# A softcap attention and max-out kernel: the first part of its written order of work made anew

## The chip, the cores and the metric

The kernel runs on one core of one Trainium2 chip. The metric is device time in microseconds (us) of one execution, the median of several. TensorE is called PE (its weight loads PEld), VectorE DVE, ScalarE ACT, GpSimd POOL, and SyncE SP, whose queue issues DMAs.

## The reference

```python
scores = scale * np.matmul(q, k.transpose(0, 1, 3, 2))      # 8 batches, 12 heads, 448 x 448, head_dim 64
scores = cap * np.tanh(scores / cap)                        # cap = 30
attn = np.exp(scores - np.max(scores, axis=-1, keepdims=True))
attn = attn / (np.sum(attn, axis=-1, keepdims=True) + 1e-09)
x = np.matmul(attn, v)                                      # heads side by side: 3584 x 768
g = np.maximum(x @ w1, x @ w2)                              # 768 -> 1024
out = g @ w_out                                             # 1024 -> 768, float32
```

## The kernel before

The heads are taken two at a time ("pairs" i, 48 of them) and the pairs two at a time ("quads" t, 24). For one pair q and k come in, are cast to bf16 and turned so that the head dimension lies on the partitions: for the first ten pairs by PE transposes, later by DMA transposes. The max-out is rewritten as max(x w1, x w2) w_out = relu(x (w1 - w2)) w_out + x (w2 w_out). So a first stage makes wd = w1 - w2 on DVE and wm = w2 w_out on PE ("premultiplication"), and the rest of the kernel uses those. The products of the max-out are "groups": stage 1 gives relu(x wd), stage 2 the output rows.

There is no scheduler at work: the string `ORDER` lists every step of the whole kernel, written out, and each step issues its instructions at once. Each engine executes its own instructions in the order of the list; an instruction waits for what it needs from other engines. The place of a step against steps of other engines has no effect, only its place among those of its own engine. The steps that matter here:

- `ld0` loads q or k of pairs 0 and 1 (k on SP's queue, q on ACT's), `cd` casts them (ACT, the very first k on DVE). `lk`, `lq`, `lv` load k, q, v, `lw1`, `lw2`, `lwo` the weights, all on POOL's queue with a cast.
- `dm` fills a tile for warming matmuls, `ms0` and `id` make the identity (DVE, then POOL), `ms` fills constants (DVE). `D b n` does warming matmuls on n blocks of 128 columns in bank b, four blocks a matmul; their result is not used.
- `Xh`, `X i b` turn pair i into bank b (PE, 28 transposes of 64 x 64), `XCh`, `XC` copy that out (DVE). `W c b` turns a piece of w2 (8 transposes), `WC` copies it out. `OP c half b` takes bank b for a premultiplication, `P c half n` does n of its 8 matmuls, `PC` copies it out.
- `S i j` are the scores of pair i, keys j (2 matmuls of 64 x 448, in one of two PSUM slots of the scores), `T` their tanh and `E` their exp (ACT). `L`, `TL`, `EL` are the same for the keys left over by 3 x 128.
- `Y` sums the exps with a matmul of ones, `Y1`, `Y2`, `Y3` invert the sums (DVE), `VL`, `V` multiply by v (in a slot of the scores), `N` normalizes (DVE; `N t 1` is two instructions). `A`, `B` add exps ahead of the sum (DVE).
- `O g b` takes bank b for group g, `M x y n` does n steps of the first 64 rows for group x and n of the other 64 rows for group y, side by side, `ev` copies a group out (DVE), `H`, `Hs` hand a bank from one half to the other, `sub` makes a piece of wd (DVE), `cr` is a DMA transpose (SP), `st` a store.

The eight PSUM banks are four for the two slots of the scores and four (0 to 3) that `X`, `W`, `OP`, `Y`, `O` and `D` share. A bank that is taken again is written only when its old content has been read; the instruction on PE waits for that.

```python
def mm_tile(bank):
    idle.pop(bank, None)
    return mm_psum.tile([P, 512], f32, name=f"mm{bank}", bufs=1)
def s_tile(turn, t):
    return s_psum.tile([P, 2, 512], f32, name=f"s{turn ^ (t % 2)}")
```

Lines of the profile: L289 to L292, L734 and L735 are `ms`, `dm`, `ms0`; L277 `id`; L303 `ld0`; L308 and L310 `cd`; L321 and L328 `lk`, `lq`; L352 `lv`; L360 `lwo`; L366 `lw2`; L393 `lw1`; L402 `sub`; L416 `W`; L420 `WC`; L431 `P`; L437 `PC`; L458 `X`; L463 `XC`; L471 `D`; L475 `cr`; L514 `S`; L519 `T`; L528 `L`; L532 `TL`; L536 `E`; L539 `EL`; L548 `A`; L553 `B`; L566, L570 and L573 `Y`; L578, L581 and L584 `Y1` to `Y3`; L600 `VL`; L606 `V`; L618 and L621 `N`; L645 `M`; L666, L700 and L702 `ev`.

Of the kernel before, what the change touches and what calls it, by code (L numbers as in the profile page):

```python
# [778 lines left out]
```

## Time and profile before

| | |
|---|---|
| median of 3 runs | 330.23 us (330.17 to 330.53) |
| profiled execution | 330.47 us, span of its trace 328.7 us |
| PE busy | 321.4 us (98%) |
| ACT busy | 281.4 us (86%) |
| DVE busy | 240.5 us (73%) |
| POOL busy | 161.8 us (49%) |
| DMA | 46.28 MB, mean 141 GB/s |

A row of a timeline has the start in us, the duration of the piece, the engine, the line, the operation, what it writes and reads with partitions x elements, the count of instructions merged into the piece, and in brackets the idle time of the engine before it and what ended that. A row of a stretch has its bounds, its length, then the busy time of each engine with the count of instructions, the granted clock, the busy share of the DMA engines and GB/s. A row of a DMA queue has packets, MB and the share of the 16 engines' time.

### The profile page before, as it was taken

Reading aid. Unit: us, or ns where it says so; the run is one execution under the profiler, and the core shown is the slowest. Engines: PE = TensorE matmul, PEld = TensorE weight load, DVE = VectorE, ACT = ScalarE, POOL = GpSimd, SP = SyncE. Lnnn points to the kernel's source line nnn. Section 1 sums busy time; section 2 is a strip of 40 time slices with the busy share of each in tenths; the row PEclk is TensorE's granted clock in tenths of the full one; section 3 lists DMA queues with packets and bytes.
Section 4 is the critical chain, followed back from the end, with each engine's and each line's share of the span. In section 5 each row is a group of like instructions: output and inputs, shape, how many; then the busy total and the mean of one; then the engine's idle time right before and its main releaser. Section 6 shows DMA issues by size and latency. Waiting matters only on the chain.

```text
span 328.7 us, 9775 instructions
## 1 busy us (share of the span) xinstructions
PE 321.4 (98%) x4139; PEld 185.1 (56%) x4139; DVE 240.5 (73%) x422; ACT 281.4 (86%) x278; POOL 161.8 (49%) x237
## 2 busy tenths in 40 slices
...
GB/s 188 200 201 224 207 161 182 107 133 122 204 184 106 104 205 196 108 111 175 164 167 70 217 138 185 112 157 157 190 114 76 216 161 47 2 50 98 0 98 96
DMA packets 134507, 46.28 MB, mean 141 GB/s; under 512 B 112320, under 2 KB 129472, under 8 KB 134464
## 3 DMA queue, kind: packets, MB, share of 16 engines
...
q10 hardware_dynamic: 448, 0.66, 0.6%
...
## 4 chain that ended last, share of the span: by engine, by line
PE 96%; DVE 2%; issue 0%
PE mm L645 61%; PE s L514 10%; PE s L606 9%; PE mm L431 4%; PE s L528 2%; PE mm L471 2%; PE mm L573 2%; PE s L600 2%; PE mm L640 1%; PE mm L458 1%; PE mm L416 1%; DVE xT L621 1%; PE mm L566 1%; DVE xT L618 0%; DVE qkT L463 0%
## 5 line engine op out<-in xcount | busy, mean ns | idle before, releaser
L519 ACT ACTIVATE e<-s 128x896 bf16<-128x896 f32 x144 | 125.7, 928 | 6.6 <-PE s L514 6.4
L536 ACT ACTIVATE e<-e 128x1792 bf16<-128x1792 bf16 (+2 forms) x72 | 122.7, 1712 | 0.0
L645 PE MATMUL mm<-wo_sb,gT 64*128 64x384 bf16 x864 | 115.2, 323 | 0.0
L645 PE MATMUL mm<-wm_sb,xT 64*128 64x384 bf16 x648 | 102.3, 322 | 0.0
L645 PE MATMUL mm<-xT,wd_sb 64*128 64x448 bf16 x768 | 97.3, 349 | 0.0
L328 POOL DMA_DIRECT2D kqs<-in_k_dram x76 | 54.7, 722 | 56.2 <-DMA qkT<-kqs 51.4
L645 PEld LDWEIGHTS <-gT 64*128 64x128 bf16 x864 | 58.7, 94 | 25.3 <-issue 0.9
L645 PEld LDWEIGHTS <-wd_sb 64*128 64x128 bf16 x768 | 48.9, 94 | 26.5 <-issue 2.0
L645 PEld LDWEIGHTS <-xT 64*128 64x128 bf16 x648 | 50.7, 94 | 18.3
L514 PE MATMUL s<-qkT 64*128 64x448 bf16 x288 | 52.8, 355 | 0.6 <-DVE xT L621 0.6
L352 POOL DMA_DIRECT2D vp<-in_v_dram x48 | 30.5, 639 | 38.2 <-PE s L514 28.0
L666 DVE TENSOR_SCALAR gT<-mm 128x448 bf16<-128x448 f32 x64 | 38.9, 617 | 8.7 <-PE mm L645 7.6
L328 POOL DMA_DIRECT2D kqs<-in_q_dram x38 | 35.1, 925 | 4.4 <-PE mm L458 2.8
L606 PE MATMUL s<-e,vp 128*32 128x448 bf16 x576 | 35.6, 354 | 0.0
L548 DVE TENSOR_TENSOR esum<-e 128x896 bf16<-128x896 bf16 x42 | 25.8, 617 | 9.9 <-ACT e L536 9.9
L621 DVE TENSOR_TENSOR xT<-s,inv 64x448 bf16<-64x448 f32 x48 | 29.9, 622 | 0.9
L548 DVE TENSOR_TENSOR esum<-esum,e 128x896 bf16<-128x896 bf16 x42 | 26.2, 623 | 5.9 <-ACT e L536 4.8
L514 PEld LDWEIGHTS <-qkT 64*128 64x128 bf16 x288 | 18.5, 94 | 20.3 <-issue 11.1
L700 ACT COPY osb<-mm 128x384 f32<-128x384 f32 x10 | 4.8, 478 | 26.9 <-PE mm L645 26.7
L702 DVE COPY osb<-mm 128x384 f32<-128x384 f32 x44 | 23.3, 553 | 5.2 <-PE mm L645 4.7
L553 DVE TENSOR_TENSOR esum<-esum,el 64x896 bf16<-64x896 bf16 x42 | 26.0, 619 | 1.2
L578 DVE STREAM_TRANSPOSE st<-mm 128x448 f32<-128x448 f32 x24 | 15.6, 649 | 13.0 <-PE mm L573 11.4
...
## 6 DMA issues: line engine op xcount, KB each, us to landing
...
```

The costliest lines, as they stand in the source:

```text
L328: nc.gpsimd.dma_start(out=to, in_=x)
L352: nc.gpsimd.dma_start(out=to, in_=x)
L514: scored[i, j] = nc.tensor.matmul(s[:, h, :S], k_of(t, o, h, j), q_of(t, o, h)).ins
L519: nc.scalar.activation(expo[i][:, 2 * j : 2 * j + 2, :], slots[i, j][:, :, :S], AF.Tanh, scale=scale / cap)
L536: nc.scalar.activation(e, e, AF.Exp, scale=float(cap))
L548: nc.vector.tensor_add(d, e[:, 0:2, :] if j == 1 else d, e[:, 2 * j : 2 * j + 2, :])
L553: nc.vector.tensor_add(d, d, left_e[t][r, :, :])
L606: nc.tensor.matmul(vals[t][place(m, u), u, :S], w[:, m, :], expo[2 * t + o][:, 2 * j + h, :], start=False, stop=(j == NJ - 1))
L621: nc.vector.tensor_mul(x[64 - r : 128 - r], vals[t][r : r + 64, u, :S], sums[t, 3][64 - r : 128 - r])
L645: ins = nc.tensor.matmul(self.ps, w[r], x[r], start=first, stop=self.at == [self.n, self.n]).ins
L666: nc.vector.tensor_relu(gT[b // 2][:, f, cs], ps)
L702: nc.vector.tensor_copy(o[:, hs], ps)
```

## The change

Only `ORDER` changes. The steps up to the first ones of group 11 (438 steps before, 428 after) stand in a new order, with new banks; behind them the steps are the same 1900, with the banks 0, 1, 2, 3 renamed to 3, 2, 0, 1. The steps of the first part are the same in kind and number, but for the warming matmuls (96 blocks of 128 columns before, 104 after) and for pieces cut differently. Among the fills, `dm` and `ms0` stand ahead of `ms`; on POOL's queue the loads of pairs 3 and 2 stand ahead of the identity, and w2 and w_out behind them. In the old order one bank is taken while the copy of its old content stands further back in the list (`OP 4 0 2` before `XC 8`); in the new one none is.

```diff
@@ ORDER @@
-ld0 q; ld0 k; ms; ms0; dm; cd k; ld0 q 1; ld0 k 1; id; lwo 0 0; lw2 3; lw2 2; lk 3 0; lq 3 0; lw2 1; lk 2 0;
-lq 2 0; cd q; D 3 24; Xh 0 0 0; Xh 0 1; cd k 1 1; cd q 1 1; XCh 0 1; XCh 0 0; D 3 4; X 1 1; S 0 0; S 0 1; D 0 5;
-XC 1; T 0 0; T 0 1; D 1 16; S 0 2; L 0; W 3 2; T 0 2; TL 0; D 1 22; S 1 0; S 1 2; D 3 1; W 2 3; EL 0; T 1 0;
-T 1 2; lwo 0 1; lq 4 0; lk 4 0; lw2 0; lv 0 0; lv 0 1; WC 3; WC 2; D 2 8; S 1 1; D 2 4; OP 3 0 0; P 3 0 4; X 3 3;
-D 1 8; D 2 2; W 1 2; D 1 2; OP 2 0 1; P 2 0 2; XC 3; X 2 3; WC 1; XC 2; P 2 0 2; OP 1 0 2; P 1 0 3; S 2 1; T 1 1;
-E 0 0 3; E 1 0 2; T 2 1; S 2 0; P 1 0 2; P 3 0 1; P 1 0 1; P 3 0 1; L 1; P 2 0 1; P 1 0 2; P 2 0 2; P 3 0 2;
-P 2 0 1; PC 1 0; PC 2 0; T 2 0; TL 1; E 1 2 3; S 2 2; S 3 0; T 2 2; T 3 0; W 0 2; X 4 1; VL 0; V 0 0 0 3; Y 0 3;
-V 0 1 0 3; S 3 1; lwo 1 0; lwo 1 1; lq 5 0; lv 1 0; lk 5 0; lv 1 1; lq 7 0; lw2 4; lq 6 0; lk 6 0; lk 7 0; lw2 5;
-lq 8 0; lk 8 0; lw1 4; WC 0; XC 4; Y1 0; Y2 0; Y3 0; N 0 0; N 0 1; PC 3 0; E 2 0 3; T 3 1; EL 1; E 3 0 2;
-OP 2 1 1; P 2 1 1; OP 0 0 2; P 0 0 1; P 2 1 1; P 0 0 3; OP 1 1 3; P 1 1 2; P 2 1 1; P 1 1 1; P 2 1 1; P 1 1 3;
-P 0 0 2; P 2 1 2; S 3 2; S 4 0; P 0 0 2; OP 0 1 0; P 0 1 2; P 2 1 1; P 1 1 2; P 2 1 1; PC 0 0; X 5 2; PC 1 1;
-PC 2 1; XC 5; T 3 2; T 4 0; E 3 2 3; lw1 2; lw1 0; lq 9 0; lv 2 1; lv 2 0; S 4 1; S 4 2; T 4 1; T 4 2; Y 1 3; L 2;
-W 4 2; OP 3 1 1; P 3 1 1; VL 1; V 1 0 0 1; V 1 1 0 2; V 1 0 1 2; V 1 1 2 3; V 1 0 2 3; Y1 1; Y2 1; Y3 1; N 1 0;
-N 1 1; WC 4; TL 2; E 4 0 3; S 5 0; X 6 3; P 3 1 7; T 5 0; EL 2; XC 6; PC 3 1; S 5 1; S 5 2; X 8 2; X 7 3; T 5 2;
-T 5 1; E 5 2 3; E 5 0 2; OP 4 0 2; P 4 0 1; W 5 1; S 6 1; S 6 0; T 6 1; T 6 0; XC 8; WC 5; sub 4 0; XC 7; P 4 0 3;
-OP 5 1 1; P 5 1 1; P 4 0 2; P 0 1 4; P 5 1 1; P 0 1 2; Y 2 3; L 3; P 4 0 1; P 5 1 1; S 6 2; P 5 1 2; P 4 0 1;
-P 5 1 2; TL 3; T 6 2; sub 2 0; PC 0 1; sub 0 0; Y1 2; Y2 2; Y3 2; PC 4 0; P 5 1 1; O 1 0; M 1 -1 1; S 7 0; VL 2;
-V 2 0 0 3; V 2 1 0 3; OP 5 0 2; P 5 0 8; N 2 0; N 2 1; PC 5 1; EL 3; E 6 0 3; T 7 0; lk 10 1; lk 9 0; lq 11 0;
-lv 5 2; lq 12 0; lw1 1; lw1 3; lk 12 0; lk 12 1; lq 10 0; lk 11 1; lv 3 1; lw1 5; lk 11 0; lk 10 0; lv 3 0; S 7 2;
-O 0 3; M 0 -1 3; S 7 1; M 0 -1 3; T 7 2; T 7 1; Hs 0; S 8 1; X 9 1; M 1 -1 2; M 1 0 3; S 8 0; A 3 0 1; PC 5 0;
-sub 1 0; XC 9; sub 3 0; A 3 0 2; T 8 1; E 7 0 2; T 8 0; O 2 1; M 2 0 3; L 4; OP 4 1 2; P 4 1 8; S 8 2; M 2 1 3;
-A 3 1 1; ev 0; B 3 0; PC 4 1; B 3 1; Hs 2; TL 4; E 7 2 3; T 8 2; S 9 0; O 3 3; M 3 1 3; M 3 2 3; O 4 2; M 4 2 3;
-T 9 0; EL 4; A 3 1 2; ev 1; sub 5 0; Hs 3; cr 5; M 4 3 1; S 9 1; Y 3 0; VL 3; V 3 1 0 1; V 3 0 0 3; V 3 1 1 3;
-M 4 3 2; lq 13 0; lv 4 0; lk 13 0; lv 5 1; lv 5 0; lk 15 0; lv 4 1; lk 13 1; lq 15 0; lk 14 0; Y1 3; Y2 3; ev 2;
-Hs 4; O 5 1; M 5 3 3; M 5 4 3; T 9 1; E 8 0 3; E 9 0 2; Y3 3; N 3 1; ev 3; Hs 5; O 6 0; M 6 4 3; M 6 5 3; S 10 0;
-O 7 3; M 7 5 3; Hs 6; N 3 0; ev 4; ev 5; S 9 2; M 7 6 3; Hs 7; T 10 0; T 9 2; S 10 2; O 8 1; M 8 6 3; M 8 7 1;
...
+ld0 k; ld0 k 1; ld0 q; ld0 q 1; dm; ms0; lk 3 0; lk 2 0; lq 3 0; id; D 3 8; ms; cd q; cd k; lq 2 0; lw2 2; lw2 3;
+lw2 1; D 3 24; Xh 0 0 0; Xh 0 1; cd k 1 1; cd q 1 1; XCh 0 1; XCh 0 0; D 3 5; X 1 1; S 0 1; S 0 0; XC 1; T 0 1;
+T 0 0; D 0 5; D 1 12; L 0; D 1 8; S 0 2; W 2 0; TL 0; T 0 2; S 1 0; X 3 2; D 1 26; X 2 1; S 1 2; T 1 0; E 0 0 3;
+T 1 2; lwo 0 0; lwo 0 1; lv 0 1; lw2 0; lv 0 0; lk 5 0; lq 5 0; lq 4 0; lk 4 0; lwo 1 0; lv 1 1; lwo 1 1; WC 2;
+XC 3; XC 2; S 1 1; W 3 3; W 1 2; D 0 16; S 2 1; WC 1; WC 3; T 1 1; E 1 2 3; T 2 1; S 2 0; OP 1 0 1; P 1 0 1;
+OP 3 0 3; P 3 0 3; OP 2 0 0; P 2 0 3; P 1 0 1; P 2 0 1; P 1 0 2; L 1; P 3 0 1; P 1 0 2; P 3 0 1; P 2 0 1; P 1 0 1;
+P 3 0 1; P 2 0 3; P 3 0 2; PC 3 0; PC 2 0; T 2 0; E 1 0 2; TL 1; EL 0; S 2 2; S 3 0; Y 0 2; P 1 0 1; W 0 0; T 2 2;
+T 3 0; VL 0; V 0 0 0 3; V 0 1 0 3; S 3 1; X 4 3; lv 1 0; lk 8 0; lw2 5; lq 6 0; lk 7 0; lk 6 0; lw2 4; lq 8 0;
+lw1 4; lq 7 0; lw1 2; lw1 0; lv 2 1; lv 2 0; WC 0; Y1 0; Y2 0; PC 1 0; Y3 0; XC 4; N 0 0; N 0 1; E 2 0 3; T 3 1;
+EL 1; E 3 0 2; X 5 0; OP 0 0 2; P 0 0 5; OP 1 1 3; P 1 1 4; P 0 0 1; OP 2 1 1; P 2 1 3; S 4 0; S 3 2; P 0 0 1;
+P 2 1 2; P 0 0 1; P 1 1 3; P 2 1 3; P 1 1 1; XC 5; PC 0 0; PC 2 1; PC 1 1; T 3 2; T 4 0; E 3 2 3; OP 3 1 2;
+P 3 1 2; S 4 1; S 4 2; Y 1 1; T 4 1; T 4 2; L 2; P 3 1 4; VL 1; V 1 0 0 3; V 1 1 0 3; TL 2; E 4 0 3; S 5 0;
+P 3 1 2; W 4 3; T 5 0; EL 2; Y1 1; Y2 1; Y3 1; N 1 0; N 1 1; WC 4; PC 3 1; X 6 1; X 8 0; S 5 1; S 5 2; W 5 2;
+XC 8; XC 6; sub 4 0; WC 5; T 5 1; T 5 2; OP 4 0 0; P 4 0 8; S 6 0; X 7 1; OP 0 1 3; P 0 1 8; S 6 1; E 5 0 2;
+T 6 0; E 5 2 3; T 6 1; PC 4 0; XC 7; sub 2 0; PC 0 1; S 6 2; OP 5 1 1; P 5 1 7; L 3; T 6 2; TL 3; E 6 0 3; Y 2 3;
+VL 2; V 2 0 0 3; V 2 1 0 3; S 7 0; OP 5 0 2; P 5 0 1; P 5 1 1; P 5 0 7; sub 0 0; Y1 2; Y2 2; Y3 2; N 2 0; N 2 1;
+PC 5 1; A 3 0 1; PC 5 0; T 7 0; EL 3; lw1 1; lk 9 0; lq 10 0; lk 11 0; lw1 3; lq 9 0; lk 11 1; lv 3 1; lq 11 0;
+lv 4 0; lv 3 0; lk 10 0; lw1 5; lk 10 1; O 0 0; M 0 -1 1; S 7 2; S 7 1; O 1 3; M 1 -1 1; M 0 -1 3; M 1 -1 1;
+M 0 -1 2; T 7 1; T 7 2; Hs 0; S 8 0; M 1 -1 1; M 1 0 3; S 8 1; X 9 2; OP 4 1 1; P 4 1 4; sub 1 0; sub 3 0; XC 9;
+E 7 0 2; T 8 1; T 8 0; P 4 1 4; L 4; O 2 2; M 2 0 2; S 8 2; M 2 0 1; M 2 1 3; A 3 0 2; A 3 1 1; B 3 1; PC 4 1;
+ev 0; B 3 0; Hs 2; TL 4; E 7 2 3; T 8 2; S 9 0; O 3 1; M 3 1 3; M 3 2 3; O 4 0; M 4 2 3; VL 3; T 9 0; E 8 0 3;
+A 3 1 2; ev 1; ev 2; sub 5 0; Hs 3; cr 5; V 3 0 0 1; Y 3 3; V 3 0 1 3; V 3 1 0 3; M 4 3 1; S 9 1; M 4 3 2; O 5 2;
+M 5 3 3; lk 12 1; lk 13 0; lv 5 3; lq 13 0; lv 6 2; lv 4 1; lv 5 1; lk 12 0; lq 12 0; lk 15 0; lq 15 0; lk 13 1;
+lq 14 0; lk 14 0; Hs 4; M 5 4 3; T 9 1; Y1 3; Y2 3; Y3 3; ev 3; N 3 1; N 3 0; Hs 5; O 6 3; M 6 4 3; M 6 5 3;
+O 7 1; M 7 5 3; S 10 0; Hs 6; ev 5; A 4 0 1; ev 4; M 7 6 3; S 9 2; Hs 7; cr 6; EL 4; E 9 0 2; T 10 0; T 9 2;
...
```

More of the change, by code (lines that the diff above doesn't have):

```diff
@@ new lines @@
+M 12 10 1; Hs 11; cr 7; M 12 10 1; M 12 11 1; B 5 0; M 12 11 1; T 12 1; M 12 11 1; S 12 2; H 10 2; B 5 1;
+M 10 11 1; T 12 2; M 10 11 5; E 11 2 3; st 0 0; M 10 11 2; O 13 0; M 13 11 1; ev 10; L 6; VL 5; A 5 1 2; TL 6;
+V 5 0 0 2; V 5 1 0 2; Y 5 3; E 12 0 3; V 5 0 2 3; V 5 1 2 3; Y1 5; S 13 0; M 13 11 1; lv 7 0; M 13 11 1; Y2 5;
+M 13 12 2; Y3 5; M 13 12 1; lv 7 1; M 13 12 3; N 5 0; M 13 12 1; lv 7 2; M 13 12 1; T 13 0; M 13 12 1; N 5 1;
+M 13 12 1; lv 7 3; M 13 12 1; O 14 3; M 14 12 2; EL 6; Hs 13; S 13 1; lk 18 0; M 14 12 1; M 14 13 1; ev 11;
@@ new lines @@
+V 6 0 0 2; V 6 1 0 2; Y 6 1; E 14 0 3; V 6 0 2 3; V 6 1 2 3; Y1 6; S 15 0; M 18 16 1; lv 8 0; M 18 16 1; Y2 6;
+M 18 17 1; Y3 6; M 18 17 1; lv 8 1; M 18 17 1; O 19 1; M 19 17 2; ev 16; Hs 18; lv 8 2; M 19 17 1; M 19 18 1;
+T 15 0; N 6 0; M 19 18 2; lv 8 3; O 20 2; M 20 18 2; EL 7; Hs 19; ev 17; M 20 18 1; lk 20 0; S 15 1; M 20 19 1;
+N 6 1; M 20 19 1; T 15 1; M 20 19 1; lk 20 1; O 21 0; M 21 19 3; Hs 20; M 21 20 1; lq 20 0; ev 18; M 21 20 1;
+S 15 2; S 16 0; ev 19; M 21 20 1; T 15 2; O 22 3; M 22 20 1; lk 21 0; M 22 20 1; A 7 0 1; Hs 21; M 22 20 1;
@@ new lines @@
+M 22 21 1; E 15 0 2; M 22 21 1; lk 21 1; ev 20; S 16 1; M 22 21 1; O 23 1; M 23 21 1; A 7 0 2; M 23 21 1; Hs 22;
+lq 21 0; M 23 21 1; M 23 22 2; ev 21; M 23 22 1; T 16 0; M 23 22 2; A 7 1 1; M 23 22 2; cr 9; M 23 22 1; T 16 1;
+M 23 22 1; B 7 0; S 16 2; M 23 22 2; B 7 1; O 24 2; M 24 22 1; T 16 2; M 24 22 2; H 23; M 24 23 1; H 22 2;
+E 15 2 3; M 24 23 2; M 22 23 1; L 8; VL 7; A 7 1 2; TL 8; V 7 0 0 2; V 7 1 0 2; Y 7 0; E 16 0 3; V 7 0 2 3;
+lk 22 0; V 7 1 2 3; Y1 7; S 17 0; M 22 23 1; lv 9 0; M 22 23 1; Y2 7; M 22 23 2; Y3 7; M 22 23 1; lv 9 1;
@@ new lines @@
+M 22 23 2; O 25 0; M 25 23 1; N 7 0; M 25 23 1; lv 9 2; M 25 23 1; T 17 0; M 25 24 1; N 7 1; M 25 24 2; lv 9 3;
+M 25 24 2; EL 8; M 25 24 1; S 17 1; lk 22 1; M 25 24 2; ev 22; M 25 24 1; T 17 1; S 17 2; lq 22 0; M 25 24 1;
+ev 23; M 25 24 1; O 26 3; M 26 24 1; T 17 2; M 26 24 1; A 8 0 1; Hs 25; S 18 0; M 26 24 1; lk 23 0; M 26 25 1;
+A 8 0 2; M 26 25 1; Hs 24 2; E 17 0 2; M 26 25 1; S 18 1; lk 23 1; M 24 25 1; Hs 26; M 24 25 4; lq 23 0;
+M 24 25 3; T 18 0; O 27 1; M 27 25 1; A 8 1 1; M 27 25 1; cr 10; M 27 25 1; M 27 26 1; ev 24; M 27 26 1; T 18 1;
@@ new lines @@
+M 27 26 1; S 18 2; ev 25; M 27 26 2; T 18 2; M 27 26 1; B 8 0; M 27 26 4; B 8 1; st 1 3; E 17 2 3; M 27 26 1;
+O 28 2; M 28 26 2; L 9; VL 8; A 8 1 2; TL 9; V 8 0 0 2; V 8 1 0 2; Y 8 0; E 18 0 3; V 8 0 2 3; V 8 1 2 3; Y1 8;
+lk 24 0; st 1 4; S 19 0; M 28 26 1; M 28 27 1; Y2 8; M 28 27 1; Hs 26 2; lv 10 0; M 28 27 1; Y3 8; M 26 27 3;
+Hs 28; lv 10 1; M 26 27 1; N 8 0; M 26 27 2; T 19 0; M 26 27 1; lv 10 2; N 8 1; M 26 27 1; O 29 0; M 29 27 3;
+EL 9; lv 10 3; M 29 28 1; S 19 1; M 29 28 2; lk 24 1; ev 26; M 29 28 1; T 19 1; S 19 2; M 29 28 1; ev 27;
@@ new lines @@
+M 29 28 1; lq 24 0; M 29 28 1; T 19 2; M 29 28 1; A 9 0 1; S 20 0; M 29 28 2; A 9 0 2; M 29 28 1; lk 25 0;
+E 19 0 2; O 30 3; M 30 28 1; S 20 1; M 30 28 1; Hs 29; M 30 28 1; lk 25 1; M 30 29 2; Hs 28 2; M 30 29 1;
+M 28 29 1; lq 25 0; M 28 29 1; T 20 0; Hs 30; M 28 29 1; A 9 1 1; M 28 29 1; cr 11; M 28 29 2; B 9 0; M 28 29 1;
+T 20 1; M 28 29 1; S 20 2; O 31 1; M 31 29 1; ev 28; M 31 29 1; T 20 2; M 31 29 1; B 9 1; M 31 30 3; st 1 5;
+E 19 2 3; ev 29; O 32 2; M 32 30 3; H 31; L 10; ev 30; VL 9; TL 10; V 9 0 0 2; A 9 1 2; V 9 1 0 2; E 20 0 3;
@@ new lines @@
+lv 12 2; N 10 1; M 40 39 3; Hs 38 2; M 38 39 1; EL 11; lv 12 3; M 38 39 1; S 23 1; M 38 39 2; lk 28 1; A 11 0 1;
+M 38 39 1; T 23 1; S 23 2; M 38 39 2; A 11 0 2; lq 28 0; M 38 39 1; T 23 2; O 41 2; M 41 39 1; S 24 0; ev 38;
+M 41 39 2; M 41 40 1; lk 29 0; E 23 0 2; M 41 40 1; ev 39; S 24 1; M 41 40 2; lk 29 1; M 41 40 5; lq 29 0;
+M 41 40 1; T 24 0; M 41 40 1; A 11 1 1; O 42 0; M 42 40 1; cr 13; M 42 40 2; H 41; B 11 0; T 24 1; M 42 41 1;
+S 24 2; M 42 41 2; H 40 2; B 11 1; M 40 41 1; T 24 2; M 40 41 5; st 2 0; E 23 2 3; M 40 41 2; O 43 1; M 43 41 1;
@@ new lines @@
+ev 40; L 12; VL 11; A 11 1 2; TL 12; V 11 0 0 2; V 11 1 0 2; Y 11 3; E 24 0 3; V 11 0 2 3; V 11 1 2 3; Y1 11;
+S 25 0; lk 30 0; M 43 41 2; Y2 11; M 43 42 2; Y3 11; lv 13 0; M 43 42 4; N 11 0; lv 13 1; M 43 42 2; T 25 0;
+M 43 42 1; N 11 1; M 43 42 1; lv 13 2; M 43 42 1; O 44 3; M 44 42 2; EL 12; Hs 43; S 25 1; lv 13 3; M 44 42 1;
+M 44 43 1; ev 41; M 44 43 1; Hs 42 2; T 25 1; lk 30 1; S 25 2; M 44 43 1; A 12 0 1; M 42 43 2; Hs 44; lq 30 0;
+T 25 2; M 42 43 1; A 12 0 2; S 26 0; M 42 43 3; E 25 0 2; M 42 43 1; lk 31 0; S 26 1; M 42 43 1; O 45 2;
@@ new lines @@
+ev 58; M 61 59 1; T 32 2; M 61 59 1; B 15 1; M 61 60 3; st 3 5; E 31 2 3; ev 59; O 62 0; M 62 60 3; H 61; L 16;
+ev 60; VL 15; TL 16; V 15 0 0 2; A 15 1 2; V 15 1 0 2; E 32 0 3; M 62 61 1; Y 15 1; V 15 0 2 3; V 15 1 2 3;
+lk 38 0; Y1 15; S 33 0; M 62 61 2; Y2 15; lv 17 0; O 63 3; M 63 61 1; st 3 6; Y3 15; M 63 61 2; Hs 62; lv 17 1;
+M 63 62 1; T 33 0; N 15 0; M 63 62 2; lv 17 2; O 64 1; M 64 62 1; ev 61; M 64 62 1; Hs 63; EL 16; M 64 62 1;
+S 33 1; lv 17 3; N 15 1; M 64 63 3; T 33 1; lk 38 1; O 65 2; M 65 63 2; Hs 64; M 65 63 1; M 65 64 1; ev 62;
```

234 lines of the change are left out of this document (95 added, 139 removed).

## The prediction

> **What bounds the kernel now.** I read the page first, then busy time by stretch, then the timelines of PE, ACT, DVE and POOL where an engine stood still, and last the DMA queues at the start.
>
> ```profile
> span 328.7 us, 9775 instructions
> PE 321.4 (98%) x4139; PEld 185.1 (56%) x4139; DVE 240.5 (73%) x422; ACT 281.4 (86%) x278; POOL 161.8 (49%) x237
> PE 96%; DVE 2%; issue 0%
> 0.00:7.50 7.50, 5.61 (x67) 2.61 (x67) 2.45 (x10) 2.88 (x4) 5.07 (x13) 1.00 0.84 192
> 7.50:33.00 25.50, 25.31 (x331) 12.56 (x330) 12.22 (x22) 24.92 (x25) 15.21 (x26) 1.00 1.23 207
> 33.00:51.00 18.00, 16.95 (x256) 8.73 (x249) 15.09 (x25) 17.05 (x17) 11.52 (x16) 1.00 1.10 183
> 51.00:90.00 39.00, 39.00 (x501) 22.55 (x500) 34.96 (x61) 38.79 (x39) 25.45 (x36) 1.00 1.25 148
> 300.00:328.70 28.70, 24.56 (x256) 15.70 (x250) 5.21 (x9) 2.87 (x6) 0.00 (x0) 1.00 0.27 70
> ```
>
> PE is busy 98% of the span and makes 96% of the chain that ends last. The last 28.7 us hold 2.87 us of ACT work, so the end is set by how early PE gets through its list. In the stretch rows the columns after the length are PE, PEld, DVE, ACT and POOL. From 51 us PE has no idle time at all; in 33 to 51 it is idle 18.00 - 16.95 = 1.05 us, in 7.5 to 33 only 0.19. But from 7.5 to 33 ACT is nearly as full (24.92 of 25.50): there the pace comes from ACT, and PE's gaps are filled with warming matmuls. Both texts name the same steps from group 11 on (about 90 us), with the four mm banks only renamed. So the change is worth what it shifts the moment at which PE comes to that point, and nothing behind it.
>
> **The first 7.5 us.**
>
> ```profile
> 0.82 0.11 DVE L289 MEMSET ones<- 128x64 bf16 x1 [0.82 <-PEq L760]
> 1.53 0.27 DVE L734 MEMSET warm<- 128x256 uint32 x1
> 1.86 2.74 PE L471 MATMUL mm<-warm 128*128 128x512 bf16 x6 [1.86 <-DVE warm L734]
> 4.05 0.53 DVE L310 CAST kqs<-kr 128x448 bf16<-128x448 f32 x1 [2.25 <-DMA kr<-in_k_dram]
> 4.63 0.95 PE L458 MATMUL mm<-ident,kqs 64*64 64x64 bf16 x28
> 5.45 0.56 ACT L308 CAST kqs<-qr 128x448 bf16<-128x448 f32 x1
> 6.06 0.95 PE L458 MATMUL mm<-ident,kqs 64*64 64x64 bf16 x28
> 6.95 0.93 PE L514 MATMUL s<-qkT 64*128 64x448 bf16 x4
> 7.54 1.73 ACT L519 ACTIVATE e<-s 128x896 bf16<-128x896 f32 x2 [1.53 <-PE s L514]
> 7.80 1.32 PE L471 MATMUL mm<-warm 128*128 128x512 bf16 x6
> 16.93 0.63 PE L458 MATMUL mm<-ident,kqs 64*64 64x64 bf16 x28
> 18.41 0.55 PE L514 MATMUL s<-qkT 64*128 64x448 bf16 x4
> ```
>
> The warming tile is filled last among the constants, at 1.53, and PE starts at 1.86. With `dm` first the fill starts at 0.82 and PE about 1.86 - (1.53 - 0.82) = 1.15. The new order puts 8 warming matmuls (32 blocks of 128) there in place of 6; at 2.74 / 6 = 0.46 us each they end near 4.8, where the six ended at 4.60. The transposes of pair 0 started at 4.63, behind the casts of the first loads. So nothing is gained directly: the cover is the wait for the loads, and without it the two added matmuls would cost 0.9 us. The waits that count come after: X 1 1 starts at 6.06 because the last cast ends at 6.01 (5.45 + 0.56), and the first tanh at 7.54.
>
> These early matmuls run at half rate, though the granted clock reads 1.00 in that stretch: 28 transposes take 0.95 us at 6.06 and 0.63 at 16.93; four score matmuls 0.93 against 0.55. The six warming matmuls of 7.80 take 1.32, not 2.74. So the full rate comes near 7.6 us, 5.7 us after PE's start. With PE starting 0.7 us earlier it may come earlier. If it comes before 6.06, X 1 1 is 0.32 shorter and the first two scores half of 0.38, together -0.5 us for the first tanh; if it comes where it did, 0.
>
> The page "TensorE: Matmul & The Clock Gate" of the Trainium skill (Part 1) says that the array starts at half clock and is released after a busy window of about 3.4 us whose phase is free-running. By that rule a start 0.7 us earlier could release at once a whole window earlier in some executions and change nothing in others; the sum would be 0.5 us lower in the first case. The trace agrees on the half rate, and cannot show the phase.
>
> The identity's `affine_select` moves on POOL behind three loads, which at some 0.56 us each (`lk 3 0` below) ends it near 2.4; it is used first at 4.63, so it costs nothing, with 2.2 us of cover. The other memsets (0.5 us) come before DVE's first cast at 4.05, for which DVE had waited 2.25, and are free. ACT's and SP's own loads keep their order on each queue.
>
> The dangerous move is on POOL. Its first DMA was held until the identity was done; now `lk 3 0; lk 2 0; lq 3 0` go out from about 0.4 us, beside the four first loads on SP's and ACT's queues.
>
> ```profile
> 1.84 0.89 POOL L360 DMA_DIRECT2D wo_sb<-in_moe_w_out_dram  x1
> 3.79 0.57 POOL L321 DMA_DIRECT2D kqs<-in_k_dram  x1
> q1 hardware_dynamic: 256, 0.41, 54.1%
> q10 hardware_dynamic: 225, 0.37, 48.8%
> q0 software_dynamic: 204, 0.16, 114.1%
> q1 hardware_dynamic: 593, 0.15, 104.0%
> q0 software_dynamic: 380, 0.05, 52.8%
> ```
>
> The q1 and q10 rows are 2.5 to 4.5 us: the first loads have all engines (481 packets in 2 us). The next q0 row is 4.75 to 5.75, when POOL's queue runs. POOL's first transfer, issued at 1.84, moves nothing before about 4.5: 2.7 us. If its first transfer needs as long when issued at 0.4, the data begins at 3.1 and three quarters of the first loads are through. The last two rows, 103 to 104.5 us, show that the queues do share: 593 packets against 380, 39% for POOL. With such a share from the start, the first loads (512 packets at 240 a us, 2.1 us) would take 2.1 / 0.61 = 3.5 us: 1.35 us later. Bounds for this term: 0 and +1.35 (at one packet each, +2.1). I take +0.4, nearest to the row of 1.84, which saw no sharing, and -0.4 for the clock, most of its 0.5, since the early start fills a stretch in which PE stood empty: the first tanh at 7.5, unchanged. Range -0.5 to +1.4.
>
> **7.5 to 33 us, where ACT sets the pace.**
>
> ```profile
> 9.46 0.92 ACT L519 ACTIVATE e<-s 128x896 bf16<-128x896 f32 x1 [0.19 <-PE s L514]
> 18.82 1.73 ACT L519 ACTIVATE e<-s 128x896 bf16<-128x896 f32 x2 [0.32 <-PE s L514]
> 32.67 0.38 PE L528 MATMUL s<-qkT 64*32 64x448 bf16 x8
> ```
>
> ACT executes the same tanh and exp in both orders up to L 2, which on PE starts at 32.67 when T 4 1 has freed its PSUM slot. It stood still twice, 0.19 + 0.32 = 0.51 us, for scores that PE did late. The new order takes L 0 ahead of S 0 2, so that TL 0 can run while S 0 2 is done, and S 2 1 and S 2 0 ahead of the eleven premultiplications that stood before S 2 1. The warming between X 1 1 and that point is 67 blocks against 68, no difference. So both stalls can go. New is S 3 2 behind N 0 1, up to 0.3 for T 3 2. W2 and W_out come later than q and k now, but so do their users, the premultiplications; I count nothing for that. The term: -0.4, range -0.6 to 0.
>
> **33 to 61 us, the bank and the slot.**
>
> ```profile
> 39.58 0.32 PE L431 MATMUL mm<-wo_sb,w2T 128*128 128x384 bf16 x1 [0.37 <-DVE qkT L463]
> 50.10 0.36 PE L514 MATMUL s<-qkT 64*128 64x448 bf16 x2 [0.61 <-DVE xT L621]
> 35.38 0.62 DVE L618 TENSOR_TENSOR xT<-s,inv 128x448 bf16<-128x448 f32 x1 [1.08 <-PE s L606]
> 36.02 1.26 DVE L621 TENSOR_TENSOR xT<-s,inv 64x448 bf16<-64x448 f32 x2
> 37.31 0.69 DVE L420 COPY w2T<-mm 128x1024 bf16<-128x1024 bf16 x1
> 38.45 0.55 DVE L437 CAST wm_sb<-mm 128x384 bf16<-128x384 f32 x1
> 48.02 1.47 PE L431 MATMUL mm<-wo_sb,w2T 128*128 128x384 bf16 x8
> 39.74 0.61 PE L416 MATMUL mm<-ident,w2b 128*128 128x128 bf16 x8
> 50.51 2.54 ACT L519 ACTIVATE e<-s 128x896 bf16<-128x896 f32 x3 [0.50 <-PE s L514]
> ```
>
> The first row is the only place in the old text where a bank is taken ahead of its copy: OP 4 0 2 while XC 8 is still to come on DVE. PE, which works in order, waited 0.37. The second is S 7 2, whose slot N 2 1 had not yet read out: 0.61. Together 0.98 of the 1.05 us.
>
> In the new order S 7 0, nine premultiplications and one M stand between V 2 and S 7 2: 9 x 1.47 / 8 + 0.55 / 2 = 1.93 us without the M, against 0.62 + 1.26 = 1.88 for N 2. That wait goes, and what is late next is S 8 0, which needs T 7 1. At the other place W 5 2 now needs PC 3 1, queued on DVE behind N 1 and WC 4: 0.62 + 1.26 + 0.69 + 0.55 = 3.1 us after V 1. PE has in between three scores, two premultiplications, W 4 and two X: 0.82 + 0.37 + 0.61 + 1.26 = 3.06. A wait of 0 to 0.3 stays; behind it stand OP 4 0, S 6 0 and ACT's T 6 0. Further on O 3 1 stands behind PC 4 1 and Y 3 3 behind ev 1, on a DVE that has 34.96 of 39 us filled; I put 0.3 there. So of 1.05 us I count -0.45 (range -1.0 to +0.3). ACT's 0.50 at S 7 2 goes with it.
>
> **Sum:** 0 - 0.4 - 0.45 = -0.85 us. The profiled execution took 330.47 us (span 328.7 and 1.77 around it), 0.24 above the median of 330.23. 330.47 - 0.85 = 329.6, on the median 329.4.
>
> **Rivals.**
> 1. The clock comes early and POOL's loads disturb nothing: the first term is -0.5 instead of 0, 328.9. For it: POOL's 2.7 us. Chance 0.15.
> 2. The waits change their place. DVE's queue holds the banks as long as before, because N, PC and the subtractions are all still there; the 1.05 us come back at W 5 2, O 3 1 and Y 3 3, and T 3 2 waits: 330.2. This is also the case in which the rule on banks does nothing, since it touched one wait of 0.37. For it: DVE's fill; against: S 7 2, whose new cover is 1.93 against 1.88. Chance 0.22.
> 3. Slower: POOL's three or four loads share the engines with the first loads. The price is 1.35 at the shares of 103 us, 2.1 at one packet each; 1.75 in the middle, less 0.85 for the other terms and no clock gain: +0.9, 331.1. It decides above 0.85 us. For it: the shares row; against: no POOL packet before 4.5. Chance 0.23.
>
> The page "DMA: Bandwidth & Descriptors" of the Trainium skill (Queues, rings and completion order) states that an engine takes turns between the queues that have work, packet by packet. By it POOL's queue would get a third beside two others and the loads would land about 1.0 us later, a sum of +0.15. The shares of 103 us agree with it, the start of this trace does not show it.
>
> **Numbers.** The forecast has 0.40, its own range 328.8 to 330.0. The measurement of this kernel can tell about 0.2%, 0.66 us, from no change. Below 329.57 lie rival 1, most of the forecast: 0.50. Above 330.89 lie most of rival 3 and a part for a late load elsewhere: 0.24. The rest, 0.26. The range goes from rival 1 with the full 1.05 us, 328.4, to rival 3, 331.2.
>
> **What would show it.** PE's first matmul near 1.15; X 1 1 at 6.1 or below (right) or beyond 6.8 (rival 3), the casts ended by DMA; 28 transposes at 0.63 or 0.95; no wait of PE on a copy near 39 longer than 0.3; S 7 2 without one; ACT's stalls of 0.19 and 0.32 gone; PE's idle time from 51 to 90 still near 0. The prediction is wrong if the first tanh moves by over 0.8 us, or if PE idles over 1 us between 33 and 61.

## The result, and the profile after

| | before | after |
|---|---|---|
| median | 330.44 us (330.17 to 331.21, 6 runs) | 329.37 us (328.85 to 329.59, 6 runs) |
| ratio | | 0.9961, 95% interval 0.9947 to 0.9975 |
| profiled execution | 330.47 us, span 328.7 | 329.59 us, span 327.8 |

The new order is about 1.1 us faster by the medians, 1.3 by the ratio, and 0.9 in the two profiled executions. Each ratio is taken against executions of the kernel before that were measured along with it, and two executions far off all others, one of before (1841.54 us) and one of b1 (547.13 us, granted clock 0.56), are left out of the ratios. The page of the kernel after (span, busy time of the engines) and its busy time by stretch, with the columns of the prediction's stretch rows:

```profile
span 327.8 us, 9768 instructions
PE 320.3 (98%) x4137; PEld 184.6 (56%) x4140; DVE 240.2 (73%) x422; ACT 281.2 (86%) x278; POOL 161.7 (49%) x237
0.00:7.50 7.50, 6.25 (x73) 2.66 (x74) 2.59 (x10) 3.47 (x5) 6.40 (x16) 1.00 0.82 191
7.50:33.00 25.50, 24.02 (x323) 12.45 (x325) 11.82 (x21) 24.40 (x26) 12.19 (x22) 1.00 1.15 175
33.00:51.00 18.00, 17.47 (x254) 8.97 (x252) 15.78 (x27) 17.63 (x18) 11.25 (x17) 1.00 1.23 230
51.00:90.00 39.00, 38.86 (x506) 22.29 (x504) 34.97 (x60) 38.84 (x39) 27.33 (x38) 1.00 1.31 149
```

PE's idle time from 33 to 51 us fell from 1.05 to 0.53. From 7.5 to 33 it rose from 0.19 to 1.48, and ACT, which sets the pace there, stood still 1.10 us instead of 0.58. The timelines of PE and of ACT after show where:

```profile
1.19 3.59 PE L471 MATMUL mm<-warm 128*128 128x512 bf16 x8 [1.19 <-DVE warm L734]
4.72 0.63 PE L458 MATMUL mm<-ident,kqs 64*64 64x64 bf16 x28
10.40 0.62 PE L416 MATMUL mm<-ident,w2b 128*128 128x128 bf16 x8 [1.15 <-DMA w2b<-in_moe_w_dram]
32.38 0.38 PE L528 MATMUL s<-qkT 64*32 64x448 bf16 x8
38.28 0.61 PE L416 MATMUL mm<-ident,w2b 128*128 128x128 bf16 x8 [0.53 <-DMA osb<-in_moe_w_dram]
49.16 0.55 PE L514 MATMUL s<-qkT 64*128 64x448 bf16 x4
90.42 0.39 PE L528 MATMUL s<-qkT 64*32 64x448 bf16 x8
```

```profile
5.55 0.56 ACT L308 CAST kqs<-qr 128x448 bf16<-128x448 f32 x1
6.91 1.73 ACT L519 ACTIVATE e<-s 128x896 bf16<-128x896 f32 x2 [0.80 <-PE s L514]
11.36 0.92 ACT L519 ACTIVATE e<-s 128x896 bf16<-128x896 f32 x1 [1.10 <-PE s L514]
49.75 1.73 ACT L519 ACTIVATE e<-s 128x896 bf16<-128x896 f32 x2 [0.21 <-PE s L514]
```

The first tanh came at 6.91 instead of 7.54, at once 0.63 us sooner. Then `W 2 0` held PE for 1.15 us at 10.40, and behind it stood `S 1 0`, for which ACT waited 1.10. In the chain of waits of the first 12 us the piece of w2 has the largest part. Its columns are start, length and what:

```profile
3.41 0.45 POOL kqs L321
3.85 6.50 DMA w2b<-in_moe_w_dram
10.35 0.05 issue
10.40 0.62 PE mm L416 x8
```

POOL issued that load at 3.85, behind four loads of k and q; it landed at 10.35. In the kernel before, the first piece of w2 was turned at 9.66 without a wait:

```profile
9.66 0.62 PE L416 MATMUL mm<-ident,w2b 128*128 128x128 bf16 x8
91.28 0.38 PE L528 MATMUL s<-qkT 64*32 64x448 bf16 x8
```

The second row is L 7 of the kernel before, a step that stands in both texts behind the reordered part; the row with 90.42 is the same step after. Between L 2 (32.67 before, 32.38 after) and L 7 the old order takes 58.61 us and the new one 58.04. So of 0.86 us at L 7, 0.29 was there at L 2 and 0.57 came behind it; from L 7 to the end of the span both take 237.4. This split is the measure that the experiments use, because the time to L 2 varies from one execution to the next while the time from L 2 to L 7 does not:

| kernel | L 2 at | L 2 to L 7 | ratio to the kernel before |
|---|---|---|---|
| before | 32.67 | 58.61 | |
| after | 32.38 | 58.04 | 0.9961 (0.9947 to 0.9975) |
| a1 | 32.19 | 58.03 | 0.9966 (0.9954 to 0.9978) |
| a2 | 31.59 | 58.02 | 0.9939 (0.9926 to 0.9952) |
| a3 | 31.88 | 58.02 | 0.9938 (0.9925 to 0.9950) |
| b1 | 33.38 | 58.61 | 1.0013 (1.0004 to 1.0022) |
| b2 | 32.98 | 58.61 | 1.0004 (0.9996 to 1.0013) |
| b3 | 32.74 | 58.21 | 0.9987 (0.9977 to 0.9998) |
| c1 | 31.48 | 57.52 | 0.9924 (0.9911 to 0.9936) |
| d | 33.94 | 58.04 | one run, 331.11 us |
| e1 | 32.34 | 58.02 | 0.9980 (0.9968 to 0.9991) |
| e3 | 31.65 | 57.53 | 0.9941 (0.9926 to 0.9956) |

Before, b2, b3 and e1 have the same steps up to L 2, and their L 2 lies between 32.34 and 32.98: so the 0.29 us between two single profiles say little, and the first part is judged by the ratios.

### The profile page after: what moved, and what is told of

Read it like the earlier page. It is cut to its first block, busy times and chain, and to the rows that moved or that the text cites. A ratio compares the mean times of both kernels' runs of the same rounds, so it can differ in the third digit from the quotient of the medians.

```text
span 327.8 us, 9768 instructions
## 1 busy us (share of the span) xinstructions
PE 320.3 (98%) x4137; PEld 184.6 (56%) x4140; DVE 240.2 (73%) x422; ACT 281.2 (86%) x278; POOL 161.7 (49%) x237
## 4 chain that ended last, share of the span: by engine, by line
PE 86%; DVE 6%; DMA 6%; POOL 1%; issue 1%; POOLq 0%; DVEq 0%
PE mm L645 58%; PE s L514 8%; PE s L606 8%; DMA w2b<-in_moe_w_dram 3%; PE mm L431 3%; DMA osb<-in_moe_w_dram 2%; PE s L528 2%; PE mm L573 1%; PE mm L640 1%; PE s L600 1%; DVE wd_sb L402 1%; PE mm L416 1%; DVE gT L666 1%; DVE xT L621 1%; POOL kqs L321 1%; PE mm L458 1%
## 5 line engine op out<-in xcount | busy, mean ns | idle before, releaser
L514 PE MATMUL s<-qkT 64*128 64x448 bf16 x288 | 51.8, 352 | 0.0
```

The lines of the kernel that those rows point to most:

```text
L514: scored[i, j] = nc.tensor.matmul(s[:, h, :S], k_of(t, o, h, j), q_of(t, o, h)).ins
```

## The experiments

A kernel whose name begins with a, c or d, and e3, starts from the kernel after; one with b, and e1, from the kernel before. Every edit is in `ORDER`; the line numbers in their traces are four or five smaller than in the two kernels.

**a1: the fills in the old order, with six warming matmuls ahead of the first transposes.** The rest, the order on POOL's queue too, stays as after.

```diff
-dm; ms0; lk 3 0; lk 2 0; lq 3 0; id; D 3 8; ms; cd q; cd k;
+lk 3 0; lk 2 0; lq 3 0; ms; ms0; dm; id; cd q; cd k;
```

> The changed kernel with the fills back in the old order (ms, ms0, dm) and with 6 warming matmuls ahead of the first transposes in place of 8. Theory A (the second weight load sets the pace: W 2 0 waits for its piece of w2 until 10.4 us, whenever the first tanh is, and the gain of the change comes from 33 to 61 us): the first tanh goes from 6.9 back to about 7.5 us, W 2 0 still starts at 10.4, ACT's wait before its fourth tanh shrinks from 1.1 to about 0.5, and the time stays that of the changed kernel, ratio to before 0.996 (within 0.0006). Theory B (the gain is the early clock): 0.6 us slower than the changed kernel, ratio 0.998.

329.43 us (329.35 to 329.62), against 329.37 after: no difference. The timelines of ACT and PE:

```profile
7.64 1.73 ACT L514 ACTIVATE e<-s 128x896 bf16<-128x896 f32 x2 [1.60 <-PE s L509]
10.21 0.62 PE L411 MATMUL mm<-ident,w2b 128*128 128x128 bf16 x8 [0.25 <-DMA w2b<-in_moe_w_dram]
38.09 0.61 PE L411 MATMUL mm<-ident,w2b 128*128 128x128 bf16 x8 [0.54 <-DVE wm_sb L432]
```

The first tanh comes 0.73 us later than after, but the piece of w2 lands no later: PE waits 0.25 for it instead of 1.15, and ACT ahead of its fourth tanh 0.18 instead of 1.10, less than the 0.5 that was expected. The early fills gained 0.7 us at the first tanh, and the load of w2 took all of it back.

**b1: the early fills alone, in the kernel before.**

```diff
-ld0 q; ld0 k; ms; ms0; dm; cd k;
+ld0 q; ld0 k; dm; ms0; ms; cd k;
...
-lq 2 0; cd q; D 3 24; Xh 0 0 0;
+lq 2 0; cd q; D 3 32; Xh 0 0 0;
```

> The kernel before with only the fills changed: dm and ms0 ahead of ms, and 8 warming matmuls ahead of the first transposes. Both theories: PE starts near 1.2 us, the first transposes run at full rate, the first tanh comes near 6.9. Theory A: W 3 2, which stands on PE behind three of the scores, waits for its piece of w2 until 9.2 or so, and what is left of the 0.6 us is lost at the waits of 39 and 50 us: 0 to -0.3 us, ratio 0.999 to 1.0. Theory B: -0.6 us or more, ratio 0.998.

331.05 us, ratio 1.0013 (1.0004 to 1.0022): slower by about 0.4, which neither theory had. Its timelines of ACT and PE:

```profile
6.80 2.66 ACT L515 ACTIVATE e<-s 128x896 bf16<-128x896 f32 x3 [0.80 <-PE s L510]
10.37 0.62 PE L412 MATMUL mm<-ident,w2b 128*128 128x128 bf16 x8 [1.41 <-DMA w2b<-in_moe_w_dram]
12.52 1.73 ACT L515 ACTIVATE e<-s 128x896 bf16<-128x896 f32 x2 [1.27 <-PE s L510]
```

The first tanh is at 6.80, 0.74 sooner than before. But `W 3 2` waits 1.41 us for its piece of w2, which landed near 10.3. POOL had issued it at 2.40, before it at 2.72; yet from 7.5 to 9.5 us POOL's queue moved less, first row before, second row b1 (packets, MB, share):

```profile
q0 software_dynamic: 188, 0.35, 108.5%
q0 software_dynamic: 150, 0.28, 102.5%
```

The engines were nearly as full, with fewer bytes. Why is left open. In b2 and b3 below, whose steps up to there are those of the kernel before, the same step waited 0.51 and 0.26 us for its piece and started at 9.97 and 9.73: in the old order, too, this load lands about when PE comes to it. What follows is that PE's earlier start is worth nothing in either order: the step behind it waits for w2.

**a2: two steps whose data is there stand ahead of `W 2 0`.** ACT's and DVE's orders are unchanged.

```diff
-S 0 2; W 2 0; TL 0; T 0 2; S 1 0; X 3 2; D 1 26;
+S 0 2; TL 0; T 0 2; S 1 0; X 3 2; W 2 0; D 1 26;
```

> The changed kernel with S 1 0 and X 3 2 on PE ahead of W 2 0 (they stood behind it). Theory A: PE does them in the 1.15 us in which it waited for w2, ACT's stall of 1.1 us before its fourth tanh goes, and 0.5 to 0.9 us of it reach the end: ratio 0.9935 to 0.995. Theory B, by which that wait lies beside other work that is late anyway: no change against the changed kernel, ratio 0.996.

328.51 us (328.40 to 329.05), 0.9 less than after by the medians and 0.7 by the ratios. Its second stretch:

```profile
7.50:33.00 25.50, 25.03 (x339) 12.80 (x344) 12.40 (x24) 25.49 (x26) 13.10 (x23) 1.00 1.18 182
```

ACT is busy 25.49 of 25.50 us. L 2 stands at 31.59, 0.79 sooner than after; the part behind it is the same 58.02.

**a3: the piece of w2 is loaded two places sooner**, ahead of k of pair 2 and q of pair 2; PE's order is that of after.

```diff
-lk 3 0; lk 2 0; lq 3 0; id; D 3 8; ms; cd q; cd k; lq 2 0; lw2 2; lw2 3;
+lk 3 0; lq 3 0; id; lw2 2; lk 2 0; D 3 8; ms; cd q; cd k; lq 2 0; lw2 3;
```

> The changed kernel with the load of the first piece of w2 two places sooner on POOL's queue (ahead of k and q of pair 2). Theory A: the piece lands about 1.1 us sooner, near 9.2, W 2 0 waits 0 to 0.2 us, and 0.5 to 0.9 us reach the end: ratio 0.9935 to 0.995. X 2 1, which needs the two loads now behind, starts at 13.4 and has room. Theory B: no change against the changed kernel, ratio 0.996.

328.44 us (328.25 to 329.07), also 0.9 less by the medians, 0.8 by the ratios. `W 2 0` on PE:

```profile
9.65 0.62 PE L411 MATMUL mm<-ident,w2b 128*128 128x128 bf16 x8 [0.57 <-DMA w2b<-in_moe_w_dram]
```

It starts 0.75 sooner, though half of its wait stays, more than I had expected. a2 and a3 touch the same wait from two sides, the reader and the load, and give the same gain: it was this wait, not the order of PE as such.

**d: half of the first loads on POOL's queue, to see when POOL's loads begin.** POOL loads k and q of pair 1 first; SP and ACT load only those of pair 0.

```diff
-ld0 k; ld0 k 1; ld0 q; ld0 q 1; dm; ms0; lk 3 0;
+ld0 k; ld0 q; dm; ms0; lk 1 0; lq 1 0; lk 3 0;
...
-Xh 0 1; cd k 1 1; cd q 1 1; XCh 0 1;
+Xh 0 1; XCh 0 1;
```

> The changed kernel with k and q of pair 1 loaded by POOL's queue (cast on the way, first on that queue) in place of SP's and ACT's with casts on ACT and DVE. It asks why POOL's transfers moved nothing before 4.5 us in any run although they were issued between 1.2 and 1.8. If the engines serve the first loads first, these are half as many, end near 3.6, and POOL's first packets come then. If POOL's queue needs its time after the launch, they come at 4.5 as before. Either way the second half of pair 1 comes later than in the changed kernel, X 1 1 too, and the time is the same or up to 1 us longer.

331.11 us. The DMA queues of d from 3.0 to 3.25 us (first two rows) and from 3.25 to 3.5 (last three), columns packets, MB, share:

```profile
q10 hardware_dynamic: 30, 0.05, 55.5%
q1 hardware_dynamic: 30, 0.05, 52.2%
q10 hardware_dynamic: 34, 0.05, 53.1%
q1 hardware_dynamic: 22, 0.03, 27.7%
q0 software_dynamic: 10, 0.01, 25.9%
```

Until 3.25 POOL's queue, q0, has no packet; when q1 runs empty it begins. In the kernel after, with twice the first loads, q0 has none before 4.5 and then these, from 4.5 to 5.0:

```profile
q10 hardware_dynamic: 80, 0.11, 61.0%
q0 software_dynamic: 45, 0.04, 49.4%
q1 hardware_dynamic: 16, 0.00, 3.4%
```

So it is not a fixed time from POOL's issue to its first data: POOL's loads began when the shorter of the two queues of first loads was nearly empty. That is why the early `lk` and `lq` did not delay the first loads. By the rule of the Trainium skill that the prediction weighed ("DMA: Bandwidth & Descriptors", Queues, rings and completion order: turns between the queues that have work) q0 should have had packets beside q1 and q10 as soon as it had work; at the start of these runs it had none, and whether its work was ready for the engines by then no run shows. And with two loads more ahead of it, w2 came later still:

```profile
11.95 0.62 PE L411 MATMUL mm<-ident,w2b 128*128 128x128 bf16 x8 [2.07 <-DMA w2b<-in_moe_w_dram]
12.91 0.92 ACT L514 ACTIVATE e<-s 128x896 bf16<-128x896 f32 x1 [2.01 <-PE s L509]
```

`W 2 0` starts 1.55 us later than after, L 2 1.56 later, and the profiled execution takes 1.52 more (331.11 against 329.59): while `W 2 0` stands ahead of `S 1 0`, a later landing of this piece comes through to the end in full.

**b3: the bank that was taken ahead of its copy, alone.** In the kernel before `W 5 1` goes ahead of `OP 4 0 2`, so PE has work until `XC 8` has read the bank.

```diff
-OP 4 0 2; P 4 0 1; W 5 1; S 6 1;
+W 5 1; OP 4 0 2; P 4 0 1; S 6 1;
```

> The kernel before with W 5 1 on PE ahead of OP 4 0 2; P 4 0 1: no bank is taken ahead of the copy of its old content any more, and nothing else changes. Theory (the rule on banks is worth its one wait at most): the wait of 0.37 us on XC 8 goes to 0 or moves to W 5 1, and 0 to 0.35 us reach the end, ratio 0.999 to 1.000. Rival (the rule carries most of the change's 1.0 us): ratio 0.998 or below.

330.19 us, ratio 0.9987 (0.9977 to 0.9998), and 58.21 from L 2 to L 7, 0.40 less. The wait is gone from PE, and with it ACT's stall of 0.45 ahead of `TL 3`; the one of 0.50 stays. The first row is the kernel before, the others are b3:

```profile
44.31 0.92 ACT L532 ACTIVATE el<-s 128x896 bf16<-128x896 f32 x1 [0.45 <-PE s L528]
39.22 0.62 PE L412 MATMUL mm<-ident,w2b 128*128 128x128 bf16 x8
39.68 0.33 PE L427 MATMUL mm<-wo_sb,w2T 128*128 128x384 bf16 x1
43.96 0.92 ACT L528 ACTIVATE el<-s 128x896 bf16<-128x896 f32 x1
50.16 2.54 ACT L515 ACTIVATE e<-s 128x896 bf16<-128x896 f32 x3 [0.50 <-PE s L510]
```

**b2: other work ahead of the score that waited for its slot, alone.**

```diff
-S 7 2; O 0 3; M 0 -1 3; S 7 1; M 0 -1 3;
+O 0 3; M 0 -1 3; S 7 2; S 7 1; M 0 -1 3;
```

> The kernel before with three steps of group 0 (O 0 3; M 0 -1 3) on PE ahead of S 7 2 in place of behind it: one of the two waits of the stretch 33 to 51 us, alone. Theory (the gain of the change behind 33 us is this cover): PE's wait of 0.61 us for N 2 1 goes, and 0.3 to 0.55 us of it reach the end, ratio to before 0.9983 to 0.9991. Rival (DVE is the bound from 51 us on, so what PE gains is lost at the copies): ratio 1.000, with new waits of PE on DVE between 51 and 61 us.

330.72 us, ratio 1.0004 (0.9996 to 1.0013); L 2 to L 7 unchanged at 58.61. PE no longer stands still at `S 7 2`, but 0.26 us two scores later; ACT stalls as long as before:

```profile
50.41 0.55 PE L510 MATMUL s<-qkT 64*128 64x448 bf16 x4
50.81 2.54 ACT L515 ACTIVATE e<-s 128x896 bf16<-128x896 f32 x3 [0.50 <-PE s L510]
51.78 0.37 PE L510 MATMUL s<-qkT 64*128 64x448 bf16 x2 [0.26 <-ACT e L515]
```

The work in front filled PE's gap, but the slot still came free with `N 2 1`, and the tanh at the same distance behind L 2. The time is that of the rival, but not its reason: the moment at which `N 2 1` has read the slot sets the tanh there. That DVE was the bound from 51 us on is not shown: PE has no new wait on DVE, and DVE's waits from 45 us on are those of the kernel before.

**e1: both, and V 2 ahead of `S 7 0` as in the new order**, so that `N 2 1` ends sooner.

```diff
-OP 4 0 2; P 4 0 1; W 5 1; S 6 1;
+W 5 1; OP 4 0 2; P 4 0 1; S 6 1;
...
-M 1 -1 1; S 7 0; VL 2; V 2 0 0 3; V 2 1 0 3; OP 5 0 2;
+M 1 -1 1; VL 2; V 2 0 0 3; V 2 1 0 3; S 7 0; OP 5 0 2;
...
-S 7 2; O 0 3; M 0 -1 3; S 7 1; M 0 -1 3;
+O 0 3; M 0 -1 3; S 7 2; S 7 1; M 0 -1 3;
```

> The kernel before with three moves in the middle: W 5 1 ahead of the bank that waited (as in b3), V 2 ahead of S 7 0, and the first M's ahead of S 7 2. Theory A (the rest of the gain between 33 and 51 us is the earlier V 2: it starts 0.28 us sooner because S 7 0, 0.28 us by its start-to-start distance, no longer stands ahead of it, so N 2 1 ends 0.28 sooner, S 7 2's slot is free sooner and ACT's stall of 0.50 falls to about 0.2): 0.37 + 0.28 = 0.65 us less than the kernel before, ratio 0.9980. Theory B (only the bank's wait counts): 0.37 us, ratio 0.9988, as in b3 (0.9987), with ACT's stall near 50 us unchanged at 0.50.

329.86 us (329.56 to 330.25), ratio 0.9980 (0.9968 to 0.9991), and 58.02 from L 2 to L 7: in size all that the new order has there, though not by the same account, since the new order has a wait of its own at `W 5 2` (c1). The two theories differ by less than the interval; the distance, 0.19 less than b3's 58.21, speaks for theory A. But its reason held only in part:

```profile
47.86 1.26 DVE L617 TENSOR_TENSOR xT<-s,inv 64x448 bf16<-64x448 f32 x2
49.18 0.36 PE L510 MATMUL s<-qkT 64*128 64x448 bf16 x1
49.37 0.54 PE L510 MATMUL s<-qkT 64*128 64x448 bf16 x3
49.77 2.54 ACT L515 ACTIVATE e<-s 128x896 bf16<-128x896 f32 x3 [0.50 <-PE s L510]
50.74 0.37 PE L510 MATMUL s<-qkT 64*128 64x448 bf16 x2 [0.26 <-ACT e L515]
```

`N 2 1` does end sooner: at 49.12, 16.78 us behind L 2, against 16.97 in b3. But only the first of `S 7 2`'s two matmuls starts then, at 49.18. The second uses the 64 rows of the three `M` steps that were put ahead; it starts behind the third of them, at 49.37, 17.03 behind L 2 as in b3 (17.02). So ACT's stall is still 0.50, and this tanh stands 17.43 us behind L 2, as in b3 (17.42): the work put ahead took what the earlier V 2 had won. The rest of PE's list is sooner, and the 0.19 appear behind that. Which of the two added moves carries them, no run separates.

**c1: a2, and the bank of `OP 4 0` after a copy that is done sooner.** The new order's own wait at `W 5 2` is named a DMA in the trace of after and a copy of DVE (`PC 3 1`) in that of a1. c1 does that copy ahead of `WC 4`, and exchanges two banks so that `OP 4 0` has one to take; the edit, against a2:

```diff
-WC 4; PC 3 1; X 6 1;
+PC 3 1; WC 4; X 6 1;
...
-OP 4 0 0; P 4 0 8; S 6 0; X 7 1; OP 0 1 3;
+OP 4 0 3; P 4 0 8; S 6 0; X 7 1; OP 0 1 0;
```

> The changed kernel with S 1 0 and X 3 2 ahead of W 2 0, and besides with PC 3 1 on DVE ahead of WC 4, and the banks of P 4 0 and P 0 1 exchanged (3 and 0), so that W 5 2 and P 4 0 find their banks read out sooner. If the wait of 0.53 us at W 5 2 is the bank (PC 3 1, on DVE behind N 1 and WC 4), it falls to 0.1 or less and 0 to 0.4 us reach the end, since ACT is nearly full there: ratio 0.9925 to 0.994. If it is the DMA that the profile of the changed kernel names at that place, W 5 2 starts no sooner and the ratio is 0.994, that of the kernel without this edit.

328.13 us (327.94 to 328.47), ratio 0.9924: the fastest of all, 1.2 us under the kernel after. The end of `PC 3 1` in after (first row), then `W 5 2` and the third stretch of c1:

```profile
37.68 0.55 DVE L437 CAST wm_sb<-mm 128x384 bf16<-128x384 f32 x1
36.78 0.61 PE L411 MATMUL mm<-ident,w2b 128*128 128x128 bf16 x8
33.00:51.00 18.00, 18.00 (x271) 9.46 (x265) 16.43 (x26) 17.93 (x18) 12.25 (x18) 1.00 1.25 238
```

PE has no gap left, and L 2 to L 7 takes 57.52, 0.50 less than in a2. No load was touched, and `W 5 2` starts 0.59 sooner behind L 2 (5.30 us against 5.89 in a2). So the wait of 0.53 was for the copy (in after it ends at 38.23, 0.05 before `W 5 2` starts), though the trace names a DMA.

**e3: c1 with the load of a3.** The edit, against c1:

```diff
-lk 3 0; lk 2 0; lq 3 0; id;
+lk 3 0; lq 3 0; id; lw2 2; lk 2 0;
...
-lq 2 0; lw2 2; lw2 3;
+lq 2 0; lw2 3;
```

> The best version so far (c1: two steps ahead of W 2 0, bank of OP 4 0 after a copy done earlier) with the piece of w2 also loaded two places sooner on POOL's queue (as in a3). If W 2 0 in c1 no longer waits for its load, the earlier load adds nothing: 328.1, ratio 0.9924. If the load still holds a later step back (W 3 3, or a premultiplication waiting for w_out), it gives 0.1 to 0.3 us more: ratio 0.9915 to 0.9921. If loading w2 ahead of k of pair 2 makes X 2 1 wait, it loses up to 0.3: ratio 0.993.

328.56 us (328.21 to 329.06), ratio 0.9941, whose interval overlaps that of c1 (0.9911 to 0.9936): no gain, and whether it is slower is unclear. Neither kernel has a wait of PE on a load. Its profile is 0.17 us later than c1's at L 2, as it is at the first tanh (7.25 against 7.08).

## Why the prediction was right, point by point

The forecast was 329.4 and the median is 329.37; the sum of -0.85 stands against -0.9 in the profiled executions. By the ratio the change is worth 1.3. The size was right, its parts were not all, and the agreement to 0.03 us is luck: it compares a forecast from 330.23, the median of three executions, with a run in which before has 330.44.

- **The first tanh: forecast unchanged, measured 0.63 sooner.** The term was the difference of two estimates. The full rate came early: the first 28 transposes took 0.63 instead of 0.95, and the scores start at 6.50 instead of 6.95 and take 0.55 instead of 0.93. That X 1 1 starts when the last cast ends was misread: after, it starts at 5.70 and that cast ends at 6.11. In before, the warming matmul ahead of it ran to about 6.1. POOL's loads, put at +0.4, cost 0.1 at most, the delay of the last of the first casts; d shows why. Rival 3 falls with that, and rival 1 describes the start, but not the time. Two steps towards that term were wrong besides: POOL issued from 1.24, not 0.4, and at 3.1 us not three quarters of the first loads were through but 154 of 576 packets in before. The 0.63 is one draw: the first tanh lies between 6.75 and 7.25 with the early fills (after, a2, a3, b1, c1, e3) and between 7.23 and 7.64 with the old ones (before, a1, b2, b3, e1).
- **7.5 to 33 us: forecast -0.4.** ACT's stalls of 0.19 and 0.32 did go; what that is worth alone, no run separates. What failed is the step "W2 and W_out come later than q and k now, but so do their users, the premultiplications; I count nothing for that". The first user, `W 2 0`, stood on PE ahead of `S 1 0`, and its load landed at 10.35: 1.15 us on PE, 1.10 on ACT. a2 and a3 put the price at 0.7 to 0.9 us. Both terms together were forecast at -0.4; the ratio, less the 0.57 behind L 2, gives -0.7 for after and -0.5 for a1, within the range that the intervals allow. Two errors of opposite sign, the early tanh not counted and the late load not counted, met: that the forecast of this part came out right is partly luck.
- **33 to 61 us: forecast -0.45, measured -0.57 from L 2 to L 7.** The wait for the bank went and was worth 0.40 (b3). The wait at `W 5 2` that the prediction named is there, but 0.53 instead of "0 to 0.3", and costs 0.50 (c1). The side of DVE was right (`PC 3 1` ended 3.14 us behind V 1, forecast 3.1); PE's cover, put at 3.06, was 2.65, since `S 5 2` ended at 37.74: the two X took 1.07 instead of 1.26, and the pieces overlap. PE's idle time from 51 to 90 is 0.14, where 0.3 was put for O 3 1 and Y 3 3. ACT's 0.50 near 50 us fell to 0.21. The 0.61 at S 7 2, taken by the prediction as PE time to be won, is none by itself (b2: no gain).
- **Rival 2**, the waits change their place: one did in part. W 5 2 now waits 0.53, and with it half of PE's gain there is gone.
- **What would show it:** PE's first matmul at 1.19, X 1 1 at 5.70, S 7 2 without a wait, PE idle 0.53 between 33 and 61 and 0.14 after 51, as said; a wait longer than 0.3 near 39 was to be absent, and 0.53 at 38.28 is there.

PE's idle time was the wrong currency in one place. b2 took away 0.35 us of it and none of ACT's stalls and gained nothing; b3 took 0.37 and 0.45 of ACT's and gained 0.40. But e1 gained 0.19 more than b3 at the same stall of ACT, and c1 0.50 over a2 while ACT's idle time from 33 to 51 us fell from 0.38 to 0.07 and PE's from 0.54 to 0: neither engine's column alone gives the gains from 33 us on, where both are nearly full.
